# A scheduler that ranks by stage and kind, against one that follows a written list of operation numbers

## The chip, the core and the metric

The kernel runs on one core of a Trainium2 chip. The core has five engines, each with a queue of its own that it works through in order: PE (TensorE, matrix products), DVE (VectorE), ACT (ScalarE), POOL (GpSimd) and SP (SyncE, which here only issues transfers). They meet through semaphores, and transfers run on 16 shared DMA engines. The metric is the device time of one execution in microseconds (us).

## The reference

An attention layer with exponential features is followed by a feed-forward layer with a residual. Batch 8, 8 heads, 576 tokens, head size 64, 128 features, model width 512, hidden width 2048.

```python
def phi(x):
    proj = np.einsum('bhsd,df->bhsf', x, w_phi)
    proj = proj - np.max(np.abs(proj), axis=-1, keepdims=True)
    return np.concatenate([np.exp(proj), np.exp(-proj)], axis=-1)
q_p, k_p = phi(q), phi(k)
kv = np.einsum('bhsf,bhsd->bhfd', k_p, v)
z = np.sum(k_p, axis=2)
num = np.einsum('bhsf,bhfd->bhsd', q_p, kv)
den = np.einsum('bhsf,bhf->bhs', q_p, z)[..., None] + 1e-06
attn = num / den                              # then heads side by side: x (8, 576, 512)
xn = (x - mean(x)) / np.sqrt(var(x) + 1e-06) * g_ln
out = x + np.maximum(xn @ w_ch1, 0.0) @ w_ch2
```

## The kernel before

**Units.** The attention is cut into 32 units (4 pairs of batches, 8 units each), numbered n from 0; a unit is two sequences of 576 tokens: eight whole tiles of 128 tokens and one "mixed" tile with the last 64 tokens of both. For a unit the kernel loads k, q and v (the main parts `qk` and `v`, 256 KB each, and the tails `qx` and `vx`, fetched for four units at a time), turns k and q (`qkT`; for units 0 to 7 on PE, with a copy out of PSUM by DVE or ACT at L844 or L846; later by transfer), multiplies by the feature weights (`pm`, `pt`, `px`), takes maxima (DVE, L1047 and L947), takes exponentials (ACT, L956 to L1111: `eb` for the keys, `ea` for the queries, `ek` and `em` for the maxima), scales v by `ek` (POOL, `scale_main`, L1074 to L1080: `vv`), forms k-features times v in the bank `n_bank` (copied to `KV` at L1149 or L1151), then the numerators (`num`, L1199), which DVE scales and sums (`numc`) and inverts (`rden`), and POOL writes to `x` (L1266).

**Feed-forward.** Tokens go in nine groups g of 512. Group 0 needs units 0 to 3. A group gets its statistics (`x_stats`, L1338, and L1350), is centred (`x_center`, xc), is turned (`xT`; for group 0 on PE at L1302, with copies at L1312 and L1314), then 16 products `first` (L1431, `hT_ps`, index jj, weights `w1`) with a relu each, and products `second` (L1463, `ch_ps`, weights `w2`). For the last groups both layers are done by a form with fewer products (`fast`, L1597, and `quick`, L1780). `w1` and `w2` come in two loads each, issued by POOL (`load_w1`, L769, and `load_w2`, L787); the first load of `w1` serves jj 0 to 7, the second jj 8 to 15; the first load of `w2` serves the first eight hidden blocks.

**What sets the order.** Nothing is issued while the Python code for a step runs: each step is added to a list `sched` of 2,199 operations (`Order.add`) with its engines, an estimate of its time, what it reads and writes, and room that it takes (PSUM banks). `Order.run` then plays the list through a model with estimated times, and emits the instructions in the order and on the engine that come out. Where an operation may run on two or three engines, the first one free takes it. Among those that are ready on an engine, the one of lowest rank goes first. A rank is a late start, worked back from the users of the operation, plus an offset from the table `OFF`, which has for each of the units a number for each kind of step. While PE has nothing ready and the model's clock is below 75 us, it is given a filler: a small product of zeros into `n_bank` (L2064, "warm-up matmul" below), unless the bank is in use.

The order that comes out is fixed in the program: on the chip each engine waits at the head of its own queue, however long that takes.

## Time and profile before

| | before |
|---|---|
| median of the runs shown | 356.88 us |
| lowest run | 356.73 us |
| profiled execution, first to last instruction | 354.4 us |
| around it (356.88 less 354.4) | 2.5 us |
| PE busy | 345.6 us, 98% |
| DVE busy | 304.8 us, 86% |
| ACT busy | 258.5 us, 73% |
| POOL busy | 189.3 us, 53% |
| warm-up matmuls (L2064) | 347 |

"Busy" is the union of an engine's instruction spans. A matmul's span includes the time until its result is out, and the next one overlaps it, so that the spacing of weight loads (PEld, one ahead of each matmul) tells better what a run of matmuls takes. PE counts as busy in warm-up matmuls too.

### The profile page before, as it was taken

The page shows a single profiled execution, that of the slowest core. Times are in us where ns is not written, and L with a number is a line of the kernel's source. Part 1 is how long each engine was busy: PE and PEld are TensorE (multiplying, and loading weights), DVE is VectorE, ACT ScalarE, POOL GpSimd, SP SyncE. Part 2 cuts the span into 40 slices and gives each one's busy share as a digit, 9 for nine tenths or more (in the row PEclk, how much of TensorE's full clock was granted, in tenths as well). Part 3 has the DMA queues.
Part 4 walks back from the last instruction along what each step waited for, and adds up shares of the span by engine and source line. Part 5 has one row for each costly group of instructions (what it writes and reads, how often), then busy time and mean ns, then how long its engine had stood idle before and what let it go on. Part 6 is the DMA issues. An engine that isn't in the chain of part 4 may idle for free.

```text
span 354.4 us, 9372 instructions
## 1 busy us (share of the span) xinstructions
PE 345.6 (98%) x3606; PEld 221.1 (62%) x3632; DVE 304.8 (86%) x664; ACT 258.5 (73%) x551; POOL 189.3 (53%) x245
## 2 busy tenths in 40 slices
PE   8998999999999999999999999999999999999995
PEld 8987955556554555455545455555555578578884
DVE  5699987899987888988979989897778799999983
ACT  4997988598997996979696975787697833656410
POOL 5499755799644873747478798355546420000000
PEclk9999999999999999999999999999999999999999
DMA  7999999899996888489729242851051005400053
GB/s 210 311 215 287 210 281 246 215 235 258 294 276 175 209 185 215 115 141 280 202 68 209 72 110 47 147 153 35 2 126 63 3 7 116 123 2 3 0 120 118
DMA packets 93676, 53.89 MB, mean 152 GB/s; under 512 B 61104, under 2 KB 88048, under 8 KB 93632
## 3 DMA queue, kind: packets, MB, share of 16 engines
q1 hardware_dynamic: 89392, 47.72, 56.5%
q0 software_dynamic: 3328, 4.49, 7.1%
q10 hardware_dynamic: 912, 1.08, 0.9%
q8 instruction: 28, 0.46, 0.5%
q14 instruction: 16, 0.13, 0.1%
HBM read 36.77 MB, written 9.44 MB: 130 GB/s over the span
## 4 chain that ended last, share of the span: by engine, by line
PE 88%; DVE 8%; ACT 2%; issue 1%; DVEq 0%; ACTq 0%
PE hT_ps L1431 29%; PE ch_ps L1463 22%; PE ch L1597 9%; PE n_bank L2064 4%; PE pm L990 4%; PE n_bank L1141 4%; PE sum L1780 4%; PE num L1199 3%; PE pt L999 2%; DVE m L1047 2%; PE n_bank L1135 1%; DVE numc L1221 1%; PE n_bank L1199 1%; DVE numc L1227 1%; PE n_bank L1205 1%
## 5 line engine op out<-in xcount | busy, mean ns | idle before, releaser
L1431 PE MATMUL hT_ps<-xT,w 128*128 128x512 bf16 x496 | 118.4, 379 | 0.0
L1463 PE MATMUL ch_ps<-w,hT 128*128 128x512 bf16 x362 | 88.9, 379 | 1.3 <-issue 0.3
L1047 DVE TENSOR_REDUCE m<-pm 128x8 f32<-128x1024 f32 x64 | 76.8, 1214 | 7.1 <-PE pm L990 6.5
L1074 POOL TENSOR_TENSOR vv<-v,ek 128x1024 bf16<-128x1024 f32 x32 | 61.1, 1910 | 33.0 <-issue 18.2
L1431 PEld LDWEIGHTS <-w 128*128 128x128 bf16 x496 | 44.2, 98 | 44.0 <-issue 0.8
L1067 ACT ACTIVATE eb<-pm 128x1024 bf16<-128x1024 f32 x64 | 64.5, 1036 | 2.4 <-DVE m L1047 2.3
L1111 ACT ACTIVATE ea<-pt 128x1024 bf16<-128x1024 f32 x64 | 63.8, 1029 | 3.0 <-PE pt L999 2.7
L1266 POOL TENSOR_TENSOR x<-numc,rden 128x128 bf16<-128x128 f32 (+1 forms) x64 | 38.9, 613 | 38.6 <-DVE rden L1233 37.4
L1441 ACT ACTIVATE hT<-hT_ps 128x512 bf16<-128x512 f32 x68 | 40.6, 597 | 24.1 <-PE hT_ps L1431 23.2
L1463 PEld LDWEIGHTS <-hT 128*128 128x128 bf16 x384 | 34.0, 98 | 34.4 <-issue 0.8
L1439 DVE TENSOR_SCALAR hT<-hT_ps 128x512 bf16<-128x512 f32 x56 | 38.5, 687 | 8.6 <-PE hT_ps L1431 8.1
L1199 PEld LDWEIGHTS <-ea 128*128 128x128 bf16 x512 | 24.6, 97 | 10.5 <-issue 1.7
L1141 PE MATMUL n_bank<-vv,eb 128*128 128x65 bf16 x512 | 26.6, 194 | 0.0
L902 POOL TENSOR_TENSOR b<-qk,one 128x1024 bf16<-128x1024 f32 x11 | 20.9, 1896 | 8.9 <-DMA qkT<-b 5.5
L2064 PE MATMUL n_bank<-wz 128*128 128x120 bf16 x347 | 25.0, 224 | 0.1
L1141 PEld LDWEIGHTS <-eb 128*128 128x128 bf16 x512 | 22.3, 98 | 4.3
L1221 DVE TENSOR_TENSOR numc<-num,em 128x390 f32<-128x390 f32 (+1 forms) x40 | 20.3, 513 | 3.3 <-PE num L1199 2.5
L2064 PEld LDWEIGHTS <-wz 128*128 128x128 bf16 x347 | 21.5, 103 | 1.6 <-issue 0.5
L1480 POOL TENSOR_TENSOR o<-o,x 128x512 f32<-128x512 f32 x14 | 16.2, 1154 | 10.5 <-ACT o L1476 10.5
L1338 DVE BATCH_NORM_STATS2 st<-x 128x6 f32<-128x512 bf16 (+1 forms) x40 | 21.3, 569 | 0.4 <-POOL x L1266 0.4
L1199 PE MATMUL num<-KV,ea 128*128 128x65 bf16 x416 | 19.4, 193 | 1.6 <-ACT KV L1151 1.3
L1227 DVE TENSOR_TENSOR numc<-numc,num 128x390 f32<-128x390 f32 (+1 forms) x40 | 20.3, 516 | 0.5
(162 smaller groups left out, 608.7 us busy)
## 6 DMA issues: line engine op xcount, KB each, us to landing
out_dram<-o SPq DMA_DIRECT2D x29, 256.0 KB, 2.6
qk<-in_k_dram SPq DMA_DIRECT2D x12, 512.0 KB, 5.0
qk<-in_q_dram SPq DMA_DIRECT2D x12, 512.0 KB, 6.0
v<-in_v_dram SPq DMA_DIRECT2D x12, 512.0 KB, 4.9
w<-in_moe_w_ch_dram POOLq DMA_DIRECT2D x4, 1024.0 KB, 11.4
qk<-in_k_dram SPq DMA_DIRECT2D x8, 256.0 KB, 6.9
qk<-in_q_dram SPq DMA_DIRECT2D x7, 256.0 KB, 7.5
v<-in_v_dram SPq DMA_DIRECT2D x7, 256.0 KB, 7.4
```

What stands on the lines that cost most here:

```text
L1047: nc.vector.reduce_max(out=m, in_=ps, axis=AX.X, apply_absolute_value=True)
L1067: nc.scalar.activation(eb, ps, AF.Exp, scale=(1.0, -1.0)[t])
L1074: eng.tensor_tensor(out=u["vv"][:, :, 0:MX, 0:D], in0=bcast(vb[:, hh, :].rearrange("p (c d) -> p c d", d=D), 1, 2), in1=bcast(e[:, :, 0:MX ...
L1111: nc.scalar.activation(u["EA"][:, t, 0:1024], u["pt"], AF.Exp, scale=(1.0, -1.0)[t])
L1141: nc.tensor.matmul(ps[:, t, c // 4, :], EB[:, t, c, :], vv[:, t, c, :], start=False, stop=(t == 0 and c == MX - 1), skip_group_check=True,)
L1199: nc.tensor.matmul(ps[t][:, i, :], ea(u, t, c), KV[:, t, c // 4, :], start=True, stop=True,)
L1266: eng.tensor_tensor(out=dst, in0=src, in1=by, op=ALU.mult)
L1431: nc.tensor.matmul(st["ps"], w1_sb[:, kc, jj * P : (jj + 1) * P], xT_bufs[g % XB][:, kc::KC, :], start=(kc == 0), stop=(kc == KC - 1),)
L1439: nc.vector.tensor_relu(h_sb, st["ps"])
L1441: nc.scalar.activation(h_sb, st["ps"], AF.Relu)
L1463: nc.tensor.matmul(ch[g, i], hT[g, jj][:, i * P : (i + 1) * P], w2_sb[:, jj, :], start=(jj == 0), stop=(jj == JC - 1),)
L2064: nc.tensor.matmul(warm, wz, wz[:, 0:WN], start=False, stop=False, skip_group_check=True)
```

## The change

The table `OFF` is gone, and with it ranks and the choice of the first free engine. In its place stands `ORDER`: for each of the five engines the numbers of its operations, written out in the order in which it has to take them. `run` takes the head of an engine's list when the model says that it is ready and there is room, and nothing else. The list thus sets both the order and the engine. The model's clock now only decides where warm-up matmuls are put in between, and for that its estimates are changed: a table `LAG` of the delay between two engines in place of one delay for all, and many durations by a few hundredths of a us. The instructions themselves are the same, apart from the engine on which a step with a choice runs, and from the number of warm-up matmuls, which is 288 in place of 347.

```diff
+LAG = {
+    ("PE", "DVE"): 0.205, ("PE", "ACT"): 0.205, ("PE", "SP"): 0.2, ("PE", "PE"): 0.0,
...
+RESERVE, SOON = 0.04, 0.23
-MIXED, STUCK = 1.5, 0.3
+MIXED, STUCK = 1.5, 0.05
-OFF = (
-    {
-        "load": 0.0, "trans": -17.5, "trans.copy": -150.8, "mixed": -0.8, "mixed.max": 0.0,
...
+ORDER = {
+    "POOL": """
+        7 20 10 31 22 86 105 160 33 129 120 194 128 193 142 207 185 147 230 231 258 278 222 272
...
     def run(self):
+        turn = {engine: [int(n) for n in text.split()] for engine, text in ORDER.items()}
+        for engine, numbers in turn.items():
+            for n in numbers:
+                self.ops[n].engine = engine
...
-            late = min((latest[o.number] for o in op.users), default=1000.0) - op.lag
-            late -= sum(us) / len(us)
-            latest[op.number] = late = late if op.due is None else min(late, op.due)
-            if isinstance(op.rank, tuple):
-                op.rank = sum(OFF[t][k] for t, k in op.rank) + late
...
+                elif place[engine] < len(turn[engine]):
+                    op = self.ops[turn[engine][place[engine]]]
+                    if op.number not in offered or (
+                        op.acquire and room[op.acquire[0]] < op.acquire[1]
+                    ):
+                        op = None
+                    else:
+                        place[engine] += 1
+                if op is None:
+                    if engine != self.filler[0] or now >= self.filler[1]:
+                        continue
+                    op = self.fill(now)
+                    op.engine = engine
...
-        return n * (cols / 2.4 + 4.0) / 1000.0
+        return n * (cols / 2.4 + (2.4 if cols > 100 else 3.7)) / 1000.0
```

Line numbers in the rows of the changed kernel below are its own: they lie 125 or 126 under those of the kernel before.

**Units 0 to 3, DVE.** What stands in DVE's row after the clearing of its buffers, before the change (`qkT_ps` and `qxT_ps` are the turned main and mixed parts in PSUM, `qkT0` to `qkT3` those of units 0 to 3 in SBUF; the reductions with `pm` are maxima of a main part, those with `px` of a mixed part):

```order
L1047 TENSOR_REDUCE m0_117<-pm_228 128x8
L1047 TENSOR_REDUCE m0_117<-pm_259 128x8
L844 COPY qkT0_141<-qxT_ps_297 128x128
L947 TENSOR_REDUCE m0_117<-px_306 128x2
L844 COPY qkT1_142<-qkT_ps_326 128x1024
L947 TENSOR_REDUCE m1_118<-px_368 128x2
L1047 TENSOR_REDUCE m1_118<-pm_371 128x8
L844 COPY qkT2_143<-qxT_ps_407 128x128
L1047 TENSOR_REDUCE m1_118<-pm_416 128x8
```

And the same stretch with the change:

```order
L718 COPY qkT0_141<-qkT_ps_197 128x512
L922 TENSOR_REDUCE m0_117<-pm_228 128x8
L922 TENSOR_REDUCE m0_117<-pm_245 128x8
L718 COPY qkT0_141<-qxT_ps_280 128x128
L718 COPY qkT1_142<-qkT_ps_282 128x1024
L718 COPY qkT1_142<-qxT_ps_300 128x128
L822 TENSOR_REDUCE m0_117<-px_302 128x2
L822 TENSOR_REDUCE m1_118<-px_324 128x2
L922 TENSOR_REDUCE m1_118<-pm_318 128x8
L718 COPY qkT2_143<-qkT_ps_361 128x1024
L718 COPY qkT2_143<-qxT_ps_380 128x128
L922 TENSOR_REDUCE m1_118<-pm_383 128x8
```

Three copies that ACT made are DVE's now: the second half of unit 0's main part, unit 1's mixed part and unit 2's main part. Further on, ahead of the first product of the feed-forward layer, the mixed parts of units 6 and 7 come to DVE too, while the copy of `KV` of unit 2 and that of unit 7's main part go to ACT, and the two reciprocals of unit 4 stand behind the copies of `xT`.

**Units 0 to 3, SP.** The loads that SP issues at the start, before (`qk0` and `v0` hold units 0 and 1, `qk1` and `v1` units 2 and 3; `qx0` the tails of units 0 to 3):

```order
L676 DMA qk0_100<-in_k_dram 128x2x256
L676 DMA qx0_88<-in_k_dram 64x4x64 x2
L676 DMA qk0_100<-in_k_dram 128x2x256
L676 DMA qk0_100<-in_q_dram 128x2x256
L676 DMA v0_101<-in_v_dram 128x2x256
L676 DMA qk1_102<-in_k_dram 128x2x256
L676 DMA qk1_102<-in_q_dram 128x2x256
L676 DMA v1_103<-in_v_dram 128x2x256
```

And with the change:

```order
L550 DMA qk0_100<-in_k_dram 128x2x256
L550 DMA qx1_89<-in_k_dram 64x4x64
L550 DMA qx0_88<-in_k_dram 64x4x64
L550 DMA qk0_100<-in_k_dram 128x2x256
L550 DMA qk0_100<-in_q_dram 128x2x256
L550 DMA qx0_88<-in_k_dram 64x4x64
L550 DMA qk1_102<-in_k_dram 128x2x256
L550 DMA qx1_89<-in_q_dram 64x4x64
L550 DMA qk1_102<-in_q_dram 128x2x256 x2
L550 DMA qk1_102<-in_k_dram 128x2x256
L550 DMA v0_101<-in_v_dram 128x2x256
```

The load of v of unit 1 (into `v0`) has moved behind q and k of units 2 and 3, two pieces of the tails of units 4 to 7 (`qx1`) have come in between, and one piece of the first tails stands behind k and q of unit 1.

**The weight loads, POOL.** What stands around the second load of `w1` and the two of `w2` before the change (`vv` with one number is one unit's scaled v; `x` and `xs` are results of units 0 to 3):

```order
L769 DMA w1_132<-in_moe_w_ch1_dram 128x4x1024
L1266 TENSOR_TENSOR x_156<-numc_785,rden_807 128x128
L1270 TENSOR_TENSOR xs_134<-numc_785,rden_807 128x64
L1266 TENSOR_TENSOR x_156<-numc_735,rden_775 128x2x3x64
L787 DMA w2_133<-in_moe_w_ch2_dram 128x8x512 x2
L1074 TENSOR_TENSOR vv_909<-v2_105,ek_895 128x2x8x64
```

And around the two loads of `w2` with the change, where the second half of `w2` is the first of them (`xc0` is centred group 0, the two `vv` numbers belong to units 5 and 6):

```order
L661 DMA w2_133<-in_moe_w_ch2_dram 128x8x512
L1141 TENSOR_TENSOR x_156<-numc_870,rden_911 128x128
L1239 TENSOR_TENSOR xc0_136<-mv_154,x_156 128x512 x3
L949 TENSOR_TENSOR vv_1160<-v2_105,ek_1151 128x2x8x64
L954 CAST vv_1160<-ek_1151 128x2x8
L955 TENSOR_TENSOR vv_1160<-vx1_107,ek_1151 128x2x130
L949 TENSOR_TENSOR vv_1200<-v0_101,ek_1189 128x2x8x64
L954 CAST vv_1200<-ek_1189 128x2x8
L955 TENSOR_TENSOR vv_1200<-vx1_107,ek_1189 128x2x130
L661 DMA w2_133<-in_moe_w_ch2_dram 128x8x512
```

The first half of `w2` is now issued behind the scaling of v of units 5 and 6; before, it went out ahead of that of unit 4. Of `w1`, the first load has moved from behind the scaling of unit 1 to behind five results of units 0 and 1, just ahead of the scaling of unit 3, and the second stands one result further back than before. On PE, the first product of the feed-forward layer is now jj 12, which needs the second load of `w1`; before, it was jj 0.

416 lines of the change are left out of this document (90 added, 326 removed), and 111 rows, old and new, of tables (OFF, ORDER).

## The prediction

> **What bounds the kernel now.** First the span by stages: length, then busy time of PE, PEld, DVE, ACT and POOL (instructions), granted clock, DMA share and GB/s.
>
> ```profile
> span 354.4 us, 9372 instructions
> 0.00:10.00 10.00, 8.95 (x121) 8.67 (x123) 5.35 (x22) 4.70 (x6) 4.55 (x12) 1.00 0.82 215
> 10.00:20.00 10.00, 9.95 (x176) 9.43 (x175) 7.97 (x14) 9.80 (x26) 5.91 (x7) 1.00 1.13 305
> 20.00:30.00 10.00, 9.31 (x182) 8.23 (x181) 9.79 (x25) 9.00 (x20) 9.02 (x17) 1.00 1.11 246
> 30.00:40.00 10.00, 8.53 (x172) 7.66 (x169) 10.00 (x27) 8.58 (x23) 7.47 (x11) 1.00 1.16 235
> 40.00:44.40 4.40, 4.29 (x89) 4.04 (x90) 4.23 (x12) 4.28 (x11) 4.40 (x6) 1.00 1.35 213
> 44.40:75.00 30.60, 30.44 (x285) 16.65 (x287) 25.75 (x50) 23.64 (x53) 19.73 (x26) 1.00 1.16 234
> 75.00:330.00 255.00, 253.50 (x2412) 148.23 (x2430) 224.84 (x481) 193.93 (x412) 138.27 (x171) 1.00 0.55 132
> 330.00:354.40 24.40, 20.60 (x189) 18.20 (x187) 16.84 (x41) 4.61 (x7) 0.00 (x0) 0.97 0.32 87
> ```
>
> From 44.4 to 330 us PE is idle for 0.16 + 1.50 = 1.7 us: that stage is PE's work laid end to end, and no order of it can gain more than those 1.7. So time is to be had ahead of 44.4, where the first feed-forward product starts, or behind the last product. PE looks busy at the front too, but with what? Its groups up to 44.4, its waits in the whole span, and weight loads of four stretches (start, length, count):
>
> ```profile
> L2064 PE MATMUL n_bank<-wz 128*128 128x120 bf16 x345 | 24.5, 224 | 0.1
> PE num L1199 <- ACT KV L1151: 1.3, 1, 1.3
> 1.00 2.82 PEld L2064 LDWEIGHTS <-wz 128*128 128x128 bf16 x28
> 3.77 0.47 PEld L829 LDWEIGHTS <-qk 128*128 128x128 bf16 x4
> 40.52 1.60 PEld L2064 LDWEIGHTS <-wz 128*128 128x128 bf16 x30
> 44.37 0.58 PEld L1431 LDWEIGHTS <-w 128*128 128x128 bf16 x4
> ```
>
> Of the 347 warm-up matmuls 345 lie ahead of 44.4. They are padding for waits: at the front PE waits for others. For whom? ACT is full from 10 to 20 (9.80 of 10), DVE from 20 to 44 (24.02 of 24.4). And DVE idles earlier, in pieces that end when PE hands it something:
>
> ```profile
> 9.21 0.22 DVE L844 COPY qkT<-qxT_ps 128x128 bf16<-128x128 bf16 x1 [0.30 <-PE qxT_ps L837]
> 9.96 0.42 DVE L947 TENSOR_REDUCE m<-px 128x2 f32<-128x256 f32 x1 [0.53 <-PE px L944]
> 11.09 0.69 DVE L844 COPY qkT<-qkT_ps 128x1024 bf16<-128x1024 bf16 x1 [0.70 <-PE qkT_ps L829]
> 12.21 0.42 DVE L947 TENSOR_REDUCE m<-px 128x2 f32<-128x256 f32 x1 [0.42 <-PE px L944]
> 14.06 0.23 DVE L844 COPY qkT<-qxT_ps 128x128 bf16<-128x128 bf16 x1 [0.20 <-PE qxT_ps L837]
> 14.76 1.23 DVE L1047 TENSOR_REDUCE m<-pm 128x8 f32<-128x1024 f32 x1 [0.47 <-PE pm L984]
> 16.12 0.43 DVE L1149 CAST KV<-n_bank 128x260 bf16<-128x260 f32 x1
> ```
>
> Those six pieces are 2.62 us. The front thus has this chain: loads and turned tiles to 15 us, then DVE without a gap to the statistics of group 0, then centring, turning and the first product:
>
> ```profile
> 39.62 2.04 POOL L1364 TENSOR_TENSOR xc<-mv,x 128x512 bf16<-128x512 f32 x2 [1.88 <-DVE mv L1350]
> 42.18 0.29 DVE L1233 RECIPROCAL rden<-numc 128x6 f32<-128x6 f32 x2
> ```
>
> Behind PE's last product a last scaling and a store remain; the new lists end on the same steps, so I take nothing there.
>
> **The change part by part.**
>
> *Warm-up matmuls.* 59 fewer. In the first stretch, ahead of unit 0's turning, 28 become 21; there each takes 2.82 / 28 = 0.10 us. The other 52 at 1.60 / 30 = 0.053 us make 2.8. Together 3.5 us that PE need not spend. This is a bound, not a gain: if nothing else comes earlier, PE waits idle in their place and the term is 0. The seven of the first stretch are worth nothing in any case: unit 0's first product stands at 3.77 after them, and 21 at 0.10 would end at 3.1, ahead of data that the old list meets without a wait.
>
> *Copies between ACT and DVE.* What they cost on either engine (min/median/max ns):
>
> ```profile
> L844 DVE COPY qkT<-qxT_ps x5: 185/216/225, 9.2 to 27.8; 128x128 bf16<-128x128 bf16 x5
> L844 DVE COPY qkT<-qkT_ps x5: 672/680/692, 11.1 to 38.7; 128x1024 bf16<-128x1024 bf16 x5
> L846 ACT COPY qkT<-qkT_ps x4: 585/797/1012, 4.5 to 22.4; 128x512 bf16<-128x512 bf16 x2, 128x1024 bf16<-128x1024 bf16 x2
> L846 ACT COPY qkT<-qxT_ps x3: 273/294/303, 11.4 to 38.8; 128x128 bf16<-128x128 bf16 x3
> ```
>
> ACT loses 0.59 + 0.29 + 1.01 = 1.9 us of copies up to 15 us, where it is the full engine; that takes the exponentials and the `ek` on which POOL waits forward. DVE's bill up to the first product: one half part (no row; between 0.22 and 0.68, 0.34 as half of the whole one), one whole part 0.68, three mixed parts 0.65, less one `KV` copy 0.43 and one whole part 0.68, less the reciprocals now behind `xT` 0.29: +0.27 us. DVE is full from 20 us on, so these 0.27 count.
>
> *Loads.* v of unit 1, 256 KB, no longer stands ahead of q and k of units 2 and 3. At the 305 GB/s of that stage that is 0.26 MB / 305 GB/s = 0.86 us earlier for them; two 64 KB tail pieces ahead cost 0.43 back, so 0.4 net, and unit 3's q comes before its k. DVE's pieces of 0.42 to 0.70 between 9 and 15 us hang on just these units, through PE.
>
> *What the front gains.* At most, all of DVE's 2.62 us are filled and 0.27 of new work is paid: 2.35. At least: no piece is filled and 0.27 is lost. I take 2.0, near the upper end, because two causes act on the same pieces (earlier data, a freed ACT) and because the padding that was cut, 2.8 us, leaves PE room for it. Of the 3.5 us cut, 1.5 then turn into PE waits ahead of the first product.
>
> *The weights.* No row shows them late now. These rows tell how long they take and who waits (POOL's issues with their median time from issue to landing: the pair of `w1`, alone in turn, then the pair of `w2`, together):
>
> ```profile
> w<-in_moe_w_ch_dram POOLq DMA_DIRECT2D x2, 1024.0 KB, 10.0
> w<-in_moe_w_ch_dram POOLq DMA_DIRECT2D x2, 1024.0 KB, 15.6
> 25.68 1.91 POOL L1074 TENSOR_TENSOR vv<-v,ek 128x1024 bf16<-128x1024 f32 x1
> 28.24 0.79 POOL L769 DMA_DIRECT2D w<-in_moe_w_ch_dram  x1
> 29.74 0.81 POOL L1266 TENSOR_TENSOR x<-numc,rden 128x384 bf16<-128x384 f32 x1
> 49.27 0.62 POOL L1080 TENSOR_TENSOR vv<-vx,ek 128x260 bf16<-128x260 f32 x1
> 62.51 0.38 PE L1463 MATMUL ch_ps<-w,hT 128*128 128x512 bf16 x1
> 66.39 0.27 PE L943 MATMUL n_bank<-wbk,qkT 128*128 128x256 bf16 x1
> 66.90 0.62 PE L990 MATMUL pm<-wbk,qkT 64*128 64x128 bf16 x16
> ```
>
> The first load of `w1` now goes out just ahead of the scaling of unit 3, which starts at 25.68, the second one result (0.81) later than before, at about 29.1. The second is now needed by the very first product, at 44.4 - 2.0 = 42.4: 13.3 us. The first of `w2` goes out behind the scaling of unit 6, which ends at 49.27 + 0.62 = 49.9, that is 5.5 us after the first product; it is needed by the first `ch_ps`, 62.51 - 44.37 = 18.1 us after it, and 0.9 later in the new list, where unit 8's mixed and main products (0.27 + 0.62) stand ahead of it: 13.5 us. A load that is alone takes 10.0, one of a pair 15.6. In the new list the four go out singly, over 3 us apart, so I take them as in time, cost 0.
>
> *The dense stage.* Same products, their order shuffled within each group. Bounds: 1.7 us of gain, and below that any wait that the order brings in; DVE at 224.84 of 255 and ACT at 193.93 leave room. I take 0.
>
> Sum: 354.4 - 2.0 = 352.4 us of span; around it lie 2.5 us (356.88 less 354.4), which stay: 354.9 us, 0.6% faster.
>
> **Rivals.**
>
> *PE is the front's clock.* If DVE's work were also better packed from 20 us on than I see, the cut padding would count in full, and the 1.3 us wait for `KV` would go: 3.5 - 0.7 + 1.3 = 4.1 us, and half of the dense stage's 1.7 with it: 352.0. For it: the one PE wait of over 1 us in the whole trace is that 1.3, so the old padding fitted its waits closely, and the new one was cut by the same kind of model. Against: the 9.79 and 10.00 of DVE. Chance 0.17.
>
> *The slow start lasts longer.* The 28 matmuls at 1.00 take 0.10 us each, those at 40.52 0.053: PE runs at half speed for the first stretch, though the granted clock reads 1.00. The new list leaves a hole of some 0.6 us in it (3.1 to 3.77). Should that put off the full speed by as much as the slow stretch lasted, 3 us, the 30 or so warm-up matmuls there take 0.05 more each and hold up what stands behind them: 1.5 us of the gain, 356.4. The Trainium skill has this as a rule, in TensorE: Matmul & The Clock Gate, section "What's actually happening": the array runs at half rate until it has been busy for one free-running window of about 3.4 us. By that rule a hole could cost one more window; the spacing of 0.10 and 0.053 agrees with its two rates, and no run here shows what a hole of 0.6 us does. Against: PE is idle in the new stretch for a sixth of it. Chance 0.08.
>
> *The weights come late: slower.* If a load takes 15.6 us even though they go out singly, since the DMA engines are at 1.16 to 1.35 of a full share from 30 to 44.4, then `w1` lands at 29.1 + 15.6 = 44.7 and the first product slips from 42.4 to 44.7, 0.3 later than now; `w2` lands 5.5 + 15.6 = 21.1 after it and is wanted at 18.1 + 0.9 = 19.0: 2.1 us of PE idle. 356.88 + 0.3 + 2.1 = 359.3. It decides from 13.3 us a load. Chance 0.12.
>
> *Nothing moves.* The first units hang on the loads alone, DVE's pieces stay, and PE idles where it was padded; +0.27 from DVE: 357.2. Chance 0.08.
>
> **How the numbers follow.** 0.55 for the forecast, whose own range is 2.35 of gain to 0.5: 354.5 to 356.4. With the rivals the range is 351.5 to 359.3: a little under the first rival, for its bounds, up to the third. A difference of 2%, 7.1 us, is about what a measurement of this kernel tells from no change. Faster by that needs under 349.7, more than the cut padding, the wait and the whole idle time of the dense stage together (354.4 - 3.5 - 1.3 - 1.7 + 2.5 = 350.4): 0.03. Slower by that needs over 364.0, twice the price of late weights: 0.05. Within: 0.92.
>
> **What would show it.** Right: the first L1306 product (the new line of L1431) starts near 42.4; DVE's idle time from 9 to 16 us falls under 1 us; PE idles 1 to 2 us more ahead of the first product. The first rival: it starts near 40.3. The second: spacing of 0.10 after 5 us. The third: PE's first product, or its first `ch_ps`, released by a transfer of `w`. The forecast is wrong if the dense stage shows over 2 us of PE waits for ACT, DVE or POOL.

## The result, and the profile after

The changed kernel takes 358.79 us (median of four runs, 358.16 to 359.75) beside 356.88 us of the kernel before on the same chip (356.73 to 357.57; one more run of it, disturbed, took 594.93 and is left out): a ratio of 1.0051, with a 95% interval from 1.0031 to 1.0072. Measured once more, among the trials, it was 359.98 beside 356.89, ratio 1.0083 (1.0066 to 1.0101). The forecast was 354.9, 0.6% faster; the change makes the kernel slower by 0.5 to 0.8%.

The profiled execution lasts 356.4 us for 354.4. Its stages, with the columns of the table shown of before:

```profile
span 356.4 us, 9202 instructions
...
10.00:20.00 10.00, 8.90 (x136) 8.01 (x138) 8.02 (x16) 8.84 (x21) 5.24 (x6) 1.00 1.14 291
20.00:30.00 10.00, 9.31 (x189) 8.45 (x190) 9.97 (x26) 9.81 (x25) 8.62 (x14) 1.00 0.92 233
...
44.40:75.00 30.60, 30.49 (x289) 16.52 (x289) 24.05 (x51) 24.39 (x56) 22.15 (x28) 1.00 1.19 267
75.00:330.00 255.00, 252.50 (x2403) 146.71 (x2418) 219.81 (x475) 187.86 (x404) 135.81 (x177) 1.00 0.56 132
330.00:356.40 26.40, 22.02 (x197) 18.95 (x194) 20.75 (x53) 3.07 (x6) 0.00 (x0) 0.97 0.30 81
```

Three things differ. The front: PE is busy 8.90 us from 10 to 20 for 9.95, ACT 8.84 for 9.80, and DVE 8.02 for 7.97: what was cut of the padding became idle time, and DVE got no more work done. The dense stage: PE idles 2.50 us from 75 to 330 for 1.50. The end: PE reaches the last products late and idles between them. The last row is 2.0 us longer than that of before, so that its sums can't be set beside the old ones; the last 24.4 us can:

```profile
332.00:356.40 24.40, 20.22 (x182) 17.49 (x179) 18.75 (x47) 1.81 (x4) 0.00 (x0) 0.97 0.32 87
```

In them DVE is busy 18.75 us for 16.84, and ACT 1.81 for 4.61. The waits of PE in the new kernel (in all, times, longest) say who holds it up:

```profile
PE n_bank L818 <- DVE numc L1102: 1.2, 1, 1.2
...
PE qxT_ps L711 <- DMA qx<-in_k_dram: 0.9, 1, 0.9
...
PE ch L1472 <- DVE o L1481: 0.5, 2, 0.3
```

Before the change the longest was the 1.3 us for `KV`, and it is gone. In its place stand one for DVE, one for a load, and small ones in the last products. By place:

**The front gains 0.34 us for 2.0.** The weight loads of PE, with the idle time ahead of one in brackets:

```profile
1.00 2.11 PEld L1939 LDWEIGHTS <-wz 128*128 128x128 bf16 x21
3.71 0.46 PEld L703 LDWEIGHTS <-qk 128*128 128x128 bf16 x4 [0.59 <-DMA qk<-in_k_dram]
4.12 2.05 PEld L1939 LDWEIGHTS <-wz 128*128 128x128 bf16 x20
...
8.07 1.42 PEld L1939 LDWEIGHTS <-wz 128*128 128x128 bf16 x25
10.56 0.10 PEld L711 LDWEIGHTS <-qx 128*128 128x128 bf16 x1 [1.07 <-issue]
...
44.03 0.58 PEld L1306 LDWEIGHTS <-w 128*128 128x128 bf16 x4
```

The first product comes at 44.03 for 44.37. The 20 warm-up matmuls at 4.12 still take 0.10 us each, where the old kernel's stood closer from 4.7 on: unit 0's second transpositions start at 6.13 for 5.77. Then unit 0's mixed products wait for the second small piece of k until 10.56, for 8.90 before the change; the new list has that piece (operation 18) in SP's sixth place for its third, behind k and q of unit 1. DVE's idle time from 9 to 16 us, 2.56 by the same windows before, is 2.10 (7.00 less 4.90 of work).

**The middle loses 1.2 us in one place**, at 231 us. DVE, POOL and PE there:

```profile
229.41 2.12 POOL L1387 TENSOR_TENSOR qk<-w 128x1024 bf16<-128x1024 bf16 x1
229.63 2.45 DVE L1387 TENSOR_TENSOR qk<-w,qk 128x1024 bf16<-128x1024 bf16 x1
232.01 0.35 DVE L1096 TENSOR_TENSOR numc<-n_bank,em 128x195 f32<-128x195 f32 x1
232.39 0.36 DVE L1102 TENSOR_TENSOR numc<-numc,n_bank 128x195 f32<-128x195 f32 x1
232.80 0.27 PE L818 MATMUL n_bank<-wbk,qkT 128*128 128x256 bf16 x1 [1.19 <-DVE numc L1102]
```

L1387 forms sums of `w2` weights, in eight pieces. Where DVE makes one with POOL idle (at 264.1 us) it takes 0.66 us; here, begun 0.2 us after POOL's, it ends only after POOL's has ended. The sums with `numc` behind it free the bank `n_bank`, and PE stands until they have. DVE's pieces in the changed kernel, with the least, middle and longest time of one in ns:

```profile
L1387 DVE TENSOR_TENSOR qk<-w x2: 662/663/664, 213.8 to 264.1; 128x1024 bf16<-128x1024 bf16 x2
L1387 DVE TENSOR_TENSOR qk<-w,qk x2: 689/1570/2451, 229.6 to 241.1; 128x1024 bf16<-128x1024 bf16 x2
```

And in the kernel before. There DVE began two of its three pieces while POOL was at one, and the third (192.2) while POOL formed a sum for the output (`o`), all at places where PE did not wait for what followed:

```profile
L1512 DVE TENSOR_TENSOR qk<-w x2: 1606/1850/2095, 187.9 to 207.1; 128x1024 bf16<-128x1024 bf16 x2
L1512 DVE TENSOR_TENSOR qk<-w,qk x1: 1386/1386/1386, 192.2 to 192.2; 128x1024 bf16<-128x1024 bf16 x1
```

**The end loses 1.4 us** in four gaps of PE. The old kernel has none there. These are weight loads again:

```profile
320.71 0.31 PEld L1472 LDWEIGHTS <-hT 128*128 128x128 bf16 x3 [0.31 <-issue]
331.56 0.75 PEld L1472 LDWEIGHTS <-v 128*128 128x128 bf16 x7 [0.38 <-issue]
336.19 0.75 PEld L1472 LDWEIGHTS <-hT 128*128 128x128 bf16 x7 [0.27 <-issue]
343.69 0.75 PEld L1472 LDWEIGHTS <-qk 128*128 128x128 bf16 x7 [0.45 <-issue]
```

1.2 + 1.4 - 0.3 makes 2.3 us, for 2.0 that the span grew; the rest is small differences the other way, not followed up.

### The profile page after: what moved, and what is told of

It reads as the page before. It is cut to its first block, busy times and chain, and to the rows that moved or that the text cites. A ratio compares the mean times of both kernels' runs of the same rounds, so it can differ in the third digit from the quotient of the medians.

```text
span 356.4 us, 9202 instructions
## 1 busy us (share of the span) xinstructions
PE 344.5 (97%) x3550; PEld 217.9 (61%) x3573; DVE 302.0 (85%) x671; ACT 249.9 (70%) x540; POOL 187.5 (53%) x250
## 4 chain that ended last, share of the span: by engine, by line
PE 80%; DVE 9%; ACT 4%; DMA 3%; issue 2%; DVEq 0%
PE hT_ps L1306 30%; PE ch_ps L1338 22%; PE ch L1472 8%; PE pm L865 4%; PE n_bank L1016 4%; PE num L1074 3%; PE pt L874 2%; DMA qx<-in_k_dram 2%; ACT eb L942 1%; PE sum L1655 1%; DVE o L1481 1%; ACT ea L986 1%; PE n_bank L1010 1%; DVE m L922 1%; PE n_bank L1939 1%
## 5 line engine op out<-in xcount | busy, mean ns | idle before, releaser
L942 ACT ACTIVATE eb<-pm 128x1024 bf16<-128x1024 f32 x64 | 63.7, 1038 | 9.1 <-DVE m L922 9.1
L1141 POOL TENSOR_TENSOR x<-numc,rden 128x384 bf16<-128x384 f32 (+1 forms) x64 | 39.0, 621 | 36.6 <-DVE rden L1108 36.5
L1316 ACT ACTIVATE hT<-hT_ps 128x512 bf16<-128x512 f32 x74 | 43.4, 608 | 16.0 <-PE hT_ps L1306 15.9
L1314 DVE TENSOR_SCALAR hT<-hT_ps 128x512 bf16<-128x512 f32 x50 | 33.8, 683 | 9.6 <-PE hT_ps L1306 9.6
L1213 DVE BATCH_NORM_STATS2 st<-x 128x6 f32<-128x512 bf16 (+1 forms) x40 | 22.2, 569 | 0.9 <-POOL x L1141 0.9
L1939 PE MATMUL n_bank<-wz 128*128 128x120 bf16 x288 | 22.2, 229 | 0.0
L1355 POOL TENSOR_TENSOR o<-o,x 128x512 f32<-128x512 f32 x15 | 17.9, 1195 | 5.2 <-ACT o L1351 4.6
L955 POOL TENSOR_TENSOR vv<-vx,ek 128x260 bf16<-128x260 f32 x32 | 19.9, 623 | 0.0
L865 PE MATMUL pm<-wbk,qkT 64*128 64x128 bf16 x448 | 19.7, 217 | 0.0
```

What stands on the lines that cost most here:

```text
L865: nc.tensor.matmul(ps[:, half * 4 + c, :], u["qkT"][rows, cols], wbk[rows, half, :], start=True, stop=True,)
L942: nc.scalar.activation(eb, ps, AF.Exp, scale=(1.0, -1.0)[t])
L1141: eng.tensor_tensor(out=dst, in0=src, in1=by, op=ALU.mult)
L1314: nc.vector.tensor_relu(h_sb, st["ps"])
L1316: nc.scalar.activation(h_sb, st["ps"], AF.Relu)
```

## The experiments

My theory after these traces had three parts: a collision of two sums (1.2 us), an order of the tail that leaves PE waiting for DVE (1.2 to 1.4), and a front held back by two things, a late start of the full clock and a late piece of k. All trials edit the changed kernel; lists are edited by moving operation numbers. Line numbers in their rows lie up to five off those of the changed kernel. Ratios are to the kernel before, run in turn with each; they are worked out over all the runs, and need not be the quotient of two medians:

| kernel | median us (lowest to highest) | ratio, 95% interval |
|---|---|---|
| changed, first time | 358.79 (358.16 to 359.75) | 1.0051 (1.0031 to 1.0072) |
| changed, `after_again` | 359.98 (358.46 to 360.86) | 1.0083 (1.0066 to 1.0101) |
| `b_list`: old order | 357.73 (357.19 to 358.04) | 1.0033 (1.0018 to 1.0048) |
| `b_held`: old order, old padding | 356.41 (356.13 to 358.06) | 0.9995 (0.9982 to 1.0009) |
| `a_port`: sum moved | 357.61 (357.02 to 359.99) | 1.0041 (1.0024 to 1.0058) |
| `a_first17`: more padding at 1 us | 359.55 (358.68 to 360.82) | 1.0085 (1.0062 to 1.0108) |
| `a_sp`: piece of k earlier | 358.38 (357.64 to 359.43) | 1.0054 (1.0039 to 1.0070) |
| `p_sp`: sum; old order of loads | 358.73 (357.25 to 359.15) | 1.0055 (1.0033 to 1.0077) |
| `c_fill`: sum; more padding at 8 us | 359.01 (358.05 to 360.01) | 1.0060 (1.0043 to 1.0076) |
| `p_w1`: sum; `w1` much earlier | 358.22 (357.82 to 358.78) | 1.0038 (1.0026 to 1.0050) |
| `p_w2`: sum; last `w2` earlier | 364.78 (361.79 to 367.04) | 1.0227 (1.0159 to 1.0294) |
| `c_front`: sum; piece of k, `w1` | 356.77 (356.33 to 358.03) | 1.0007 (0.9997 to 1.0017) |
| `a_tail`: old tail from operation 1934 | 359.67 (358.79 to 361.55) | 1.0094 (1.0072 to 1.0117) |
| `p_relu`: sum; six ReLUs to ACT | 357.45 (356.81 to 359.83) | 1.0032 (1.0014 to 1.0051) |
| `p_tail`: sum; old tail from 316 us | 359.41 (358.20 to 360.15) | 1.0066 (1.0050 to 1.0081) |
| `c_tail`: sum; six numbers | 359.38 (358.41 to 360.44) | 1.0066 (1.0051 to 1.0081) |
| `c_all`: `c_front` and `c_tail` | 357.66 (356.74 to 359.05) | 1.0026 (1.0014 to 1.0037) |
| `c_best`: `c_front`, old tail | 357.75 (357.12 to 360.45) | 1.0040 (1.0019 to 1.0061) |
| `c_relu`: `c_front`, six ReLUs | 356.69 (355.95 to 358.64) | 1.0005 (0.9991 to 1.0019) |

### Is it the order, or the new scheduler?

`b_list` writes the old order of each engine into the lists of the new scheduler.

> The changed kernel's scheduler, with the order that every engine had in the kernel before written out as its list (a control: list and scheduler are new, the order is old; only the number of warm-up matmuls differs, 363 for 337, since the new cost model puts other gaps into the plan). Theory (only the order counts, not how it is come by): as the kernel before, 356.2 to 357.2, with its first feed-forward product at 44.4 and no wait of TensorE for a load. Rival (the new scheduler itself costs something, by its warm-up matmuls or by the order in which the program is emitted): over 357.6.

357.73: the rival. The first product came at 46.06, the rest took as long as before (305.6 us to PE's last group of products, 305.5 before). Only warm-up matmuls differed, so `b_held` took them out of the plan and set those of before, number and place:

```diff
         for op in done:
+            if op.number < 0:
+                continue
...
                 op.emit()
+            for _ in range(FILLS.get(op.number, 0)):
+                self.filler[3]()
```

> The changed kernel's scheduler with the order of before as its lists, and with the warm-up matmuls of before, number and place (337): every engine has the same instructions in the same order as before. Theory (the 26 more warm-up matmuls held products back in the front: 41 for 33 in one place alone took 0.4 us): the same as before within 0.1%, 356.4 to 357.1. Rival (the scheduler's other order of emission across engines costs it): 357.4 to 358.0, as the control without held matmuls.

356.41 beside 356.74 of before: the same. So the lists as such cost nothing, and 26 more warm-up matmuls, in other places, cost 0.4% (1.0033 for 0.9995; the first product comes at 46.06 for 44.84). `FILLS` holds their counts by operation. One place where they keep ready products waiting, in `b_list` and then in `b_held`, 41 for 33:

```profile
39.15 2.20 PEld L1939 LDWEIGHTS <-wz 128*128 128x128 bf16 x41
```

```profile
38.18 1.78 PEld L1943 LDWEIGHTS <-wz 128*128 128x128 bf16 x33
```

`p_w1` and the trials with c have the padding held at that of the changed kernel. `p_sp` and `p_w2` have not: their traces show 29 and 50 warm-up matmuls more than the changed kernel's, and what these cost them is not shown.

### The sum of w2 at 229.6 us

```diff
 "DVE"
-  1506 1692 1551 1552 1546 1563 1547 1553 1548 1512
+  1506 1551 1552 1546 1563 1547 1553 1548 1692 1512
```

> The changed kernel with one number moved in VectorE's list: the sum of w2 (1692) that took 2.45 us beside GpSimd's sum at 229.41 is issued eight places later, behind 1548, when GpSimd's sum is over. Theory (two sums of w2 at the same time on VectorE and GpSimd: VectorE comes through only when GpSimd is done, and the divisors of unit 24 behind it are late for the products into n_bank): the sum takes 0.66 to 0.75 us in its new place, TensorE's wait of 1.2 us at 231.2 goes, and 0.9 to 1.3 us of the time with it: 357.5 to 357.9 for 358.79. Rival (the wait comes back within the next units, since VectorE works without a break there): the wait at 231 goes but others of 0.3 to 0.8 us each come between 232 and 250; time 358.4 to 358.8.

The theory, in the trace. The sum and the operations with `numc` for which PE had waited:

```profile
232.05 0.55 DVE L1098 TENSOR_TENSOR numc<-numc,num 128x390 f32<-128x390 f32 x1
232.52 0.31 DVE L1104 RECIPROCAL rden<-numc 128x3 f32<-128x3 f32 x2
232.75 0.66 DVE L1383 TENSOR_TENSOR qk<-w,qk 128x1024 bf16<-128x1024 bf16 x1
```

0.66 us for 2.45; the wait of 1.2 us is gone from PE's waits, no other came for it, and PE's last group of products starts 1.1 us earlier (350.75 for 351.87). The wait stands in all five profiled executions of the new lists without this move, and in none of the twelve with it. The other sum of this kind takes 1.74 us here for 0.69, beside POOL's `o`, and PE does not wait for it. In the time the gain is less clear: the ratio is 1.0041, clear of the 1.0083 measured later for the changed kernel and not of the 1.0051 measured first. Single runs reached 359.99: something else scatters. Among the next trials stood the changed kernel once more, for its own scatter:

> The changed kernel as it is, beside the next two, so that their differences are from one chip. The account so far (sum of w2 1.2, tail 1.2, loads between 45 and 63 up to 1.0 in some executions, front 0.3 the other way) wants 358.0 to 358.8 beside 356.5 of the kernel before, and a spread over 1.0 between its lowest and its highest time.

It was 359.98, over the range: the account lacked something that this profiled execution (span 356.7, its 358.46 the lowest of the six) does not have. The mean granted clock on record for each run tells part of it: the three slowest (360.23 to 360.86) had 0.995, the other three 0.999 or 1.000.

### The front

First the clock. `a_first17` gives the first stretch 28 warm-up matmuls again, so that no hole is left (`FIRST` 17 for 10).

> The changed kernel with seven more warm-up matmuls ahead of the lists (FIRST 17 for 10), so that its first stretch has 28 again, as before. Theory (the hole of 0.74 us in the first stretch, 2.97 to 3.71, puts the full clock off from 4.70 to 6.90): TensorE works on from 1.0 to 3.7, the granted clock stands in the record from about 4.7, the warm-up matmuls after the first transpositions come at 0.05 to 0.07 us for 0.10, and unit 0's second transpositions and its first products start about 0.4 and 1.1 us earlier (5.8 and 5.4 for 6.13 and 6.55). Of the front as a whole between 0.2 and 1.0 comes back, as far as the late piece of k does not hold the mixed products anyway: 357.8 to 358.6 for 358.79. Rival (the hole only moves warm-up work about; the data of the loads set the front): the clock stands earlier, the first product stays at 44.0 within 0.1, and the time at 358.8.

Nearer to the rival, though the first product and the time lie outside its numbers. The hole is gone and the full clock starts earlier (5.6 us for 6.9), but the time is no better than the changed kernel's. In this execution q of unit 0 landed 1.1 us later than in the changed kernel's, and the first product came at 45.18. And the hole is not what sets the clock. In `b_list`, with no hole:

```profile
1.00 2.82 PEld L1939 LDWEIGHTS <-wz 128*128 128x128 bf16 x28
3.77 0.47 PEld L703 LDWEIGHTS <-qk 128*128 128x128 bf16 x4
4.19 2.16 PEld L1939 LDWEIGHTS <-wz 128*128 128x128 bf16 x21
```

0.10 us each up to 6.3, as with the hole. The trace's record of the full clock begins between 4.1 and 7.4 us in the twenty profiled executions; at 4.1, 4.7, 5.6 and 6.8 in the four without a hole, at 4.6 to 7.4 in the others. It differs from execution to execution, whatever the list. The Trainium skill has that in TensorE: Matmul & The Clock Gate, section "What's actually happening": the window in which activity is watched runs freely, and the start of the full rate varies with it. The page gives 0.5 us either way; these executions differ by 3.3 us. My second rival's mechanism falls with this.

Then the loads. `a_sp` exchanges two numbers in SP's list:

```diff
 "SP"
-  12 48 16 27 29 18 36
+  12 16 18 27 29 48 36
```

> The changed kernel with the first six loads of SP in the order they had before: the second small piece of k of units 0 to 3 (number 18) in third place, that of units 4 to 7 (number 48) in sixth. Theory (the late piece held unit 0's mixed products, 10.56 for 8.90, and through them its exponentials and the first kv products): TensorE's wait of 0.9 us for the qx load goes, the mixed products of unit 0 start at about 9.3 (the slow clock stays), and the first feed-forward product comes 0.5 to 1.5 us earlier than 44.03; 357.3 to 358.3. Rival (VectorE is the clock of the front from 18 us on, and had caught up by 18.6 in the changed kernel): the mixed products come earlier and VectorE starts earlier by as much, but the first product moves by under 0.3 us; 358.5 to 358.8.

Between the two: unit 0's mixed products started at 8.90 and no wait for `qx` was left, but the first product stood at 44.25, and a later wait of 0.9 us for a load came in this execution:

```profile
62.56 0.28 PE L814 MATMUL n_bank<-wbk,qkT 128*128 128x256 bf16 x1 [0.93 <-DMA qkT<-b]
```

Its ratio is 1.0054, below the 1.0083 of `after_again` but not below the 1.0051 measured first, so that a gain in time is not shown. The old order of all loads of the first eight units, with the moved sum:

> The kernel with the moved sum of w2, and SP's loads of the first eight units in the order that they had before (the small pieces of k, q and v of units 4 to 7 behind the large ones again). Theory (256-byte rows make each small piece as long as a large one, 0.7 us of the queue for a quarter of the bytes; ahead of the large ones they hold back units 2 and 3, so VectorE stays without work in the front as it did before): VectorE idles under 5.5 us of the first 20 for 6.25, the first feed-forward product comes at 42.5 to 43.6 for 43.94, and 356.2 to 357.2 follows for 357.61. Rival (the list of the compute engines was made for the new order of the loads: with the old one they wait at other places): the first product at 44 to 46, 357.6 to 359.5.

The rival, by its numbers: the first product at 44.15, 358.73. That the new lists of the compute engines do not go with the old order of loads is one reading; the 29 warm-up matmuls more are another.

What does the late piece do to the scatter? The profiled executions with piece 18 in SP's sixth place show a wait of PE for it of 0.5 to 2.6 us, eleven of eleven; the nine with it in third place show none. How long differs by execution, and a long one costs more than itself. `p_tail` (whose edit lies at 316 us) had the longest. Its weight loads, and its stages with the granted clock third from the end:

```profile
7.45 1.42 PEld L1939 LDWEIGHTS <-wz 128*128 128x128 bf16 x25
11.58 0.10 PEld L711 LDWEIGHTS <-qx 128*128 128x128 bf16 x1 [2.71 <-issue]
11.62 0.85 PEld L703 LDWEIGHTS <-qk 128*128 128x128 bf16 x8
```

```profile
10.00:11.40 1.40, 0.00 (x0) 0.00 (x0) 0.00 (x0) 0.00 (x0) 0.00 (x0) 0.99 1.17 199
11.40:14.80 3.40, 2.97 (x23) 2.61 (x25) 1.57 (x4) 1.08 (x3) 0.00 (x0) 0.50 1.11 293
14.80:20.00 5.20, 5.20 (x87) 4.81 (x85) 4.20 (x7) 4.92 (x16) 2.89 (x4) 1.00 1.14 266
```

After 2.7 us without work TensorE gets half its clock for 3.4 us, and its first product comes at 46.40 for 43.94 in `a_port`, 2.5 us later. The same happened in `c_tail` behind a gap of 2.35 us (46.21), and not behind gaps of up to 2.0 us. Over all the runs of the new lists, leaving out `c_fill` and `p_w2`, the mean clock shows such a loss (0.993 to 0.995) in 18 of 61 with the piece in sixth place and in 1 of 58 with it in third; within a kernel the median of those that lost it is 0.8 to 2.4 us above that of the others. If the lost clock were all of the scatter, more padding there should cure it; `c_fill` has 40 for 25:

> The kernel with the moved sum of w2, the warm-up matmuls held at the number and places of the changed kernel, but 40 for 25 of them behind unit 0's second transpositions (91), where TensorE waits for the late small piece of k (number 18). Theory (the spread: where that piece lands late, TensorE stands idle over 1.5 us between 9 and 12, and the throttle takes half of its clock for the next 3.4 us): TensorE's wait for qx falls from 0.6 to 1.9 to under 0.7 us, no time lies more than 1.5 above the lowest, and the lowest is that of the kernel without the added matmuls, 357.0. Rival (the spread comes from the loads themselves, here and at 45 to 63, and warm-up matmuls do nothing for them, or hold the piece's products back): lowest to highest stays over 2.0, or the lowest rises by 0.3 to 0.8.

The rival: 358.05 to 360.01, though none of the six lost clock (0.999 or 1.000). The padding does not help the time; the piece must come earlier. `c_front` sees to that, and moves the `w1` loads up:

```diff
 "SP"
-  12 48 16 27 29 18 36
+  12 16 18 27 29 48 36
 "POOL"
-  105 160 33 129 120 194 128 193 142 207 185 147 230
+  105 160 142 33 129 120 194 128 193 207 147 185 230
```

> The kernel with the moved sum of w2, SP's second small piece of k (number 18) in third place and that of the later units (48) in sixth, and GpSimd's w1 loads earlier (142 behind 160, 147 behind 207), the warm-up matmuls held. Theory (the loads' order is what the change lost in the front): no wait of TensorE for qx, unit 0's mixed products at about 9, the loads of units 8 and on from 40 us, no wait of GpSimd for q or v between 44 and 63; the middle 356.6 to 357.3 and the spread under 1.2, for 357.6 and 3.0. Rival (VectorE is at work without a break from 20 us on, whatever the order of the loads): the spread narrows but the first product stays at 43.8 to 44.5, and the middle at 357.3 to 358.2.

356.77, ratio 1.0007, from 1.0041: the order of the loads is worth 0.3%. Not every wait went. PE no longer stands for the piece, but for a k near 14 us (0.9) and for a q here:

```profile
8.72 0.10 PEld L715 LDWEIGHTS <-qx 128*128 128x128 bf16 x1
8.82 0.23 PEld L707 LDWEIGHTS <-qk 128*128 128x128 bf16 x4
10.01 0.23 PEld L707 LDWEIGHTS <-qk 128*128 128x128 bf16 x4 [0.96 <-DMA qk<-in_q_dram]
```

Transfers are needed as they land, one after the other, and in the profiled execution (357.49, above the median) the first product stands at 44.42: the rival's mechanism. The median is the theory's, the spread (1.7 us) is not. Which of the two moves did it, or whether it takes both, is not shown: `a_sp` has the piece alone and gains nothing that is clear, `p_w1` has the `w1` loads alone and gains nothing, and GpSimd's waits for v and q, of which the next part tells, are still 1.0 and 0.8 us here. Nor is the lost clock all of it: the ten runs of `a_port` that kept the clock have a median of 357.47.

### The weights and the loads behind them

In the traces of the new lists the loads of units 8 and on go out 0.1 us after the second `w1` load has landed (41.6 for 41.5 in the changed kernel), and the new list issues both `w1` loads later (26.08 and 30.23 us for 19.26 and 28.24) and the last of `w2` at 48.92 for 31.4. GpSimd waits for v and q once each between 44 and 63 us, 1.0 and 0.8 us. `p_w2` moves the last `w2` load up in POOL's list (161 behind 166):

> The kernel with the moved sum of w2 (the one that took 1.2 us off), and in GpSimd's list the last load of w2 (number 161) directly behind the one ahead of it (166), where it stood before the change: it is issued near 37 us for 48.9. Theory (in the changed kernel the last load of w2 goes out at 48.9 beside the loads of q and k of the next units, those then land as they are needed, and TensorE, ScalarE and GpSimd wait for them between 44 and 63 in some executions): GpSimd's waits for q and v of 0.8 and 1.0 us in that stretch go, TensorE shows none for a load, and the times lie closer together, 356.9 to 357.5 with under 1 us between the lowest and the highest, for 357.02 to 359.99 over 12 runs. Rival (GpSimd waits in its list until the load can be issued, and its copies and sums behind it come late): GpSimd has a gap of several us near 37, and the time is 358 to 361.

Slower by 2%, but not by the rival: POOL issues both `w2` loads at 37.0 us without a gap. The loads of q that follow suffer. Issues from 36 to 60 us, KB each and median time to landing, in `p_w2`, then in the changed kernel (8.4 in `a_port`), then the stages of `p_w2` behind them:

```profile
qk<-in_q_dram SPq DMA_DIRECT2D x2, 512.0 KB, 12.1
```

```profile
qk<-in_q_dram SPq DMA_DIRECT2D x2, 512.0 KB, 7.4
```

```profile
60.00:64.70 4.70, 2.28 (x53) 2.16 (x51) 0.00 (x0) 0.19 (x1) 4.70 (x5) 1.00 0.45 75
64.70:68.10 3.40, 3.40 (x31) 1.69 (x29) 2.26 (x3) 1.50 (x3) 1.58 (x3) 0.50 1.00 307
```

PE idles half of 60 to 64.7, and pays with its clock again. Of the 50 warm-up matmuls more, 41 stand right ahead of that wait; but the first product is already 1.6 us later than in `a_port` (45.55), so that the 2% are not all the load's. For this order an early place of the load brings nothing. `p_w1` moves the `w1` loads instead, to 142 behind 105 and 147 behind 207:

> The kernel with the moved sum of w2, and in GpSimd's list the two w1 loads that it issues (142 and 147) as far ahead as before the change: 142 behind 105, 147 behind 207. The number and places of the warm-up matmuls are held at those of the changed kernel. Theory (the loads of units 8 and on are held until the second w1 load has landed, 41.5 for 38.2 before the change; they go out from 41.6 for 39.2, and land as they are needed): the first load of units 8 and on is issued near 39, GpSimd's waits of 0.8 and 1.0 us for q and v between 44 and 63 go, and the times lie closer together, with the lowest as it was: 356.9 to 357.5 in the middle, under 1.2 between lowest and highest, for 357.61 and 3.0. Rival (the bytes of w1, 2 MB, only push aside the loads of units 3 to 7, which the order of the change needs early): the front is late by 0.5 to 2 us, 358 to 359.5.

Half and half: the held loads go out from 39.5 for 41.6, GpSimd's waits go, and the times lie within 1.0 us (five runs). (In `c_front` they go out from 39.5 too, and the waits stay, so the hold alone does not make them.) But POOL has to stand for 2.7 us before it can issue the first, its work for a `vv` comes late behind that, and PE waits 1.3 us for it until 25.8, so that nothing is left in the median. POOL's row, and PE's wait:

```profile
22.32 0.78 POOL L647 DMA_DIRECT2D w<-in_moe_w_ch_dram  x1 [2.73 <-PE px L823]
```

```profile
PE n_bank L1014 <- POOL vv L959: 1.3, 1, 1.3
```

### The tail

`a_tail` goes over to the old order of every engine at operation 1934; its rows part from those of the changed kernel from 287 us on.

> The changed kernel up to 298 us; from the first operation of the last feed-forward group on (operation 1934), every engine follows the order, and has the operations, that it had before the change. Theory (the tail lost 1.2 us: six of the wide ReLUs went from ScalarE to VectorE, VectorE is busy 20.8 of the last 26.4 us for 16.8 of 24.4, and TensorE waits for its results): TensorE's gaps at 320.3, 331.1, 335.8, 339.6 and 343.2 (0.30, 0.37, 0.26, 0.08, 0.43 us) go, and 1.0 to 1.4 us of the time: 357.4 to 357.8. Rival (the gaps are latency of the products themselves, or the old order does not fit behind the new one): the gaps move to other places and 358.4 to 359.2 stays.

The rival, by its second half: the gaps at 320 to 343 went, and two came at the seam, near 294 and 295 us:

```profile
PE ch L1467 <- DVE o L1476: 1.4, 2, 0.9
```

`p_relu` gives six ReLUs back to ACT:

```diff
 "ACT"  (2053 behind 2052, 2079 behind 2074, 2098 ahead of 2116,
         2103 ahead of 2112, 2127 and 2128 behind 2124)
```

> The kernel with the moved sum of w2, and six ReLUs of the last feed-forward group (2053, 2079, 2098, 2103, 2127, 2128) on ScalarE, which had them before, instead of VectorE; the order is otherwise that of the change. Theory (in the last 26 us VectorE is the engine that TensorE waits for, 20.8 us busy of 26.4, while ScalarE has gaps of 2 to 4 us): the gaps of TensorE at 331, 336, 340 and 343 (0.37, 0.26, 0.08 and 0.43 us) shrink to under 0.5 together; 0.5 to 1.0 us off 357.61. Rival (the gaps come from the order of TensorE's own list, where a product follows the result that it needs by one group of 0.87 us): they stay as they are, and 357.4 to 357.8.

PE's time from 300 us on shrinks by 0.23 us in the profile: the second gap shrinks by 0.11 us, and in place of the last comes one of 0.38 for ACT; the ratios, 1.0032 for 1.0041, overlap in their intervals. `p_tail` tries the old order from 316 us on, where the work done so far is nearly the same.

> The kernel with the moved sum of w2, and from 316 us on (behind operation 2057 of TensorE's list, where the operations done so far differ by nine between the two orders, for seventeen at 298) every engine in the order, and with the operations, of before the change. Theory (the tail's 1.2 us is its order, and the earlier try lost at its seam: two waits of 0.9 and 0.5 us near 293 behind it): TensorE's gaps from 320 on go, no new one above 0.3 us comes, and 0.9 to 1.3 us of 357.61 go with them: 356.3 to 356.8. Rival (the tail is bound by the latency of its chain of products, sums and ReLUs in either order): 357.2 to 357.8.

The four gaps go, 1.35 us by the spacing of the products, and 1.8 come at the seam (besides the front of that execution, above). `c_tail` moves six numbers:

```diff
 "PE"
-  2068 2045 2067    ...  2114 2107 2120 2099
+  2068 2067 2045    ...  2114 2120 2107 2099
 "DVE"
-  2115 2121 2102    ...  2148 2149 2150 2153 2162 2166 2154 2152 2164
+  2102 2115 2121    ...  2149 2150 2162 2153 2154 2166 2148 2152 2164
```

> The kernel with the moved sum of w2, and in the last 36 us six numbers in other places: of TensorE's list 2067 ahead of 2045 and 2120 ahead of 2107; of VectorE's 2102 ahead of 2115, and 2148, 2152 and 2164 behind 2154. Warm-up matmuls held. Theory (each gap is one place: a product behind the ScalarE or VectorE result that it needs, with nothing between; or results behind sums that nobody waits for): the gaps at 319.2, 330.0, 334.7 and 342.0 (0.30, 0.36, 0.26 and 0.43 us) shrink by 0.8 to 1.3 together, none over 0.25 comes new, and 356.3 to 356.9 comes out for 357.6. Rival (the chain of sums through VectorE is the limit): what goes in one place comes back in the next, less than 0.4 in all.

The rival: from 315 us on PE takes 0.6 us longer. Three of the four gaps stay as they were, the last shrinks from 0.44 to 0.20, and a sum comes late for PE that did not before:

```profile
PE sum L1659 <- DVE late L1676: 0.7, 1, 0.7
```

`c_all` adds `c_front`:

> All of it: the moved sum of w2, the loads of c_front, the six numbers of c_tail, warm-up matmuls held. Theory (the three places are independent of each other, and with them the change keeps what it gains in the front): 355.4 to 356.4, below the kernel before at 356.5 to 356.9, with a spread under 1.2. Rival (the front gains nothing, by VectorE): 356.4 to 357.2, the same as before.

1.0026, with the same 0.7 us in the tail: the front's repair stands, the tail's doesn't. And the old tail once more, with three of DVE's sums drawn ahead of six others at the seam:

> The kernel with the moved sum of w2 and the loads of c_front, and from 316 us on the order of before the change, with VectorE's sums 2040, 2042 and 2059 ahead of the six sums of the weights (1989, 1993, 1991, 1995, 1990, 1994) that held them up at the seam. Theory (the tail's loss is its order): TensorE's wait of 1.7 us at 319 falls under 0.3, the gaps at 320 to 343 stay away (1.36 together), and 355.4 to 356.2 comes out for 356.77, 0.2 to 0.4% below the kernel before. Rival (VectorE's work is the tail's bound in either order): the wait shows up again at another place, 356.6 to 357.3.

The rival again; the wait comes a few products later:

```profile
322.15 0.60 PE L1659 MATMUL sum<-ea,b 128*128 128x256 bf16 x4 [1.77 <-DVE hT L1676]
```

At last the six ReLUs with `c_front`:

> c_front with the six ReLUs of the last group (2053, 2079, 2098, 2103, 2127, 2128) on ScalarE. Theory (VectorE is what the tail waits for, and 1.9 us less of it is worth the 0.2 us seen before): 356.3 to 356.8, ratio 0.998 to 1.001. Rival (the 0.2 were chance): as c_front, 356.6 to 357.0.

356.69 for 356.74 of before, ratio 1.0005: with the sum and the loads repaired, the new order is as fast as the old one, and nothing tried is clearly faster. The profile of this run (356.64, near its median) says how the two balance: the first product comes at 43.81, 0.56 us ahead of before, and from there PE takes 1.04 us longer to its last product. What the tries at the tail agree on is that a gap closed in one place came back in another; that this goes with the work that DVE has left at 316 us is argued, not shown, and which order of the tail would be without gaps stays open.

## Why the prediction was wrong

**What bounds the kernel: right.** PE's work end to end behind 44.4, DVE without a gap from 20 on: the new trace shows both again (9.97 and 10.00 of DVE from 20 to 40; from 40 to 44.4 it now has 0.7 us idle). Of the span, forecast 2.0 us shorter and measured 2.0 longer, the front accounts for 1.7 of the miss, the dense stage for 1.2 and the end for 1.4; small differences take 0.3 back.

**The front: the steps that failed are "Loads" and, built on it, "What the front gains".** The first counted q and k of units 2 and 3 as 0.4 us earlier and gave the move of piece 18 no price. In the new trace k and q of unit 2 land at 11.80 and 13.07 for 12.40 and 13.09 before, k and q of unit 3 at 14.72 and 13.82 for 14.78 and 15.54: unit 2 is complete no earlier. The small pieces it priced by their bytes, 0.21 us each; piece 18 lands at 10.34, 0.7 us behind q of unit 1 (9.63), with one small piece of POOL's in between (9.97), so 0.34 to 0.37 us each there. And piece 18, which unit 0 needs first, had moved behind k and q of unit 1. "Two causes act on the same pieces" then took 2.0 of at most 2.35; DVE's idle time fell by 0.46 (2.56 to 2.10) and the first product by 0.34, nearer to the lower bound (0.27 lost). With piece 18 back in third place (`a_sp`) PE waits for q instead, and DVE's idle time from 9 to 16 us is 2.14: what would fill it stays open.

**The padding: half right.** That 52 fewer at 0.053 need not be a gain held: they became idle time (up to 44.4 PE is busy 39.49 us for 41.04; that is within the 1 to 2 us more of waiting that the prediction named). But the term was bounded at zero on the other side, and `b_held` shows that misplaced padding costs its length. "The seven of the first stretch are worth nothing" held in `a_first17`.

**The weights: right.** No product waited for `w`. The price of two loads together that the third rival feared is real (12.1 us for q in `p_w2`), but the new list doesn't have them together.

**The dense stage, "I take 0": wrong by 1.2.** The bound was one-sided, "1.7 us of gain, and below that any wait that the order brings in", and no wait was priced. The row was there: three sums of `w2` at 1.39 to 2.10 us on DVE, each beside a sum on POOL, though alone one takes 0.66 (which only the changed kernel shows); the new list issues DVE's between 213.8 and 264.1 us for 187.9 to 207.1, one of them where a unit's bank hangs on it. `a_port` shows in the trace that this is the wait.

**The end, "the new lists end on the same steps, so I take nothing there": wrong by 1.4.** It looked at the last step and not at the 24 us ahead of it, where DVE now has 1.9 us more to do and ACT 2.8 less. That the new order leaves the gaps is shown; that DVE's load is their only cause is not, since `p_relu` took six ReLUs off it for 0.2 us.

**The rivals.** "The weights come late" gave 359.3, near the time by chance; its mechanism wasn't there. "Nothing moves" (357.2) had the front nearly right. (The bound of 364.0 for slower by 2% is three times the price of late weights, 2.4 us, and not twice.) Of the signs named, the first product at 44.03 and DVE idle for 2.10 us and not under 1 told at once that the front had failed. The sign set for the dense stage, 2 us of waits, was too coarse: one of 1.2 did the damage.

## What to carry over

An order that a model has made tight pays for every wait that the model leaves out: look for operations whose duration hangs on what another engine does at the time (the sums of `w2`: 1.39 to 2.10 us in the old trace, 0.66 to 2.45 in the new), and see what stands behind each in the new order. Price a load by its place in the queue and by who needs it first, not by its bytes alone. And padding is work: where it is planned by a model, hold its number and place fixed before blaming the order.

## What the hardware showed that I had not expected

A sum of two bf16 tiles in SBUF on DVE (128x1024) takes 0.66 us with POOL idle and 2.45 us when POOL began such a sum 0.2 us earlier. The Trainium skill says in the GPSIMD Engine Reference, section "1. Specifications", that GpSimd's SBUF interfaces are shared with VectorE, with contention where a DVE instruction has two SBUF inputs; the trace agrees, and adds that here DVE hardly moves on until POOL is done (229.41 + 2.12 = 231.53, and DVE ends at 232.08, 0.55 later). The same 0.55 us stands behind all three of DVE's sums in the kernel before and behind the one of 1.74 us in `a_port`. It can go the other way: at 241.08 in the changed kernel DVE began 0.04 us ahead of POOL's `o` and took 0.69 us, and POOL took 1.66 for the 1.16 of the same step in `a_port`.

TensorE without work for 2.35 and 2.7 us near 12 us (`c_tail`, `p_tail`) and for 2.5 us ahead of 63.9 (`p_w2`) lost half its clock for the next 3.4 us; gaps of up to 2.0 us in the front cost no clock. In the 3.41 us ahead of each loss PE was busy for 0.99 to 1.16 us; in the two executions with gaps of 2.0 us (`after_again`, `a_first17`) it was busy for 1.51 and 1.58 us of the like stretch, counted in steps of 3.41 us from the start of the full clock. Where between the two the limit lies, no run here shows. And the time at which the full clock begins differs by 3.3 us between executions of nearly the same front.
